# One-token attention with gMLP on one core: the gMLP's end moved between the first turn's quarters, the first turn's maximum behind the second turn's first product, and the last weight load cut at other rows

## The chip, the core and the metric

The kernel runs on one core of a Trainium2 chip. The metric is the device time of one execution, in microseconds (us). Before the change three runs gave 663.72, 664.41 and 665.36 us, median 664.41 us.

## What is computed

```python
xn = layernorm(x)                                  # x: 4 batches x 1 token x 640
q = (xn @ wq)                                      # 32 heads of 128
p = softmax(q . k_cache * 128**-0.5)               # 4096 keys for each batch and head
A = (p @ v_cache).reshape(4, 1, 4096) @ wo
z = gelu(xn @ w_in)                                # 640 -> 1728
z1, z2 = z[..., :864], layernorm(z[..., 864:])
B = (z1 * (w_sp[0, 0] * z2 + b_sp[0])) @ w_out     # 864 -> 640
out = x + A + B
```

All inputs are bf16. The two caches hold 4 x 32 x 4096 x 128 values each, 134 MB each; everything else together is about 14 MB.

## The kernel before, in words

**Turns.** The 32 heads and 4 batches are worked in 16 turns (`NT`); turn i takes one batch and 8 heads. Its keys, called K*i* here, are 8.4 MB, laid as 128 partitions of 256 keys with 128 numbers each. They are cut into four *quarters*. Its values, V*i*, are also 8.4 MB and are cut into two *parts*.

**Buffer.** SBUF holds one `ring` of 11 units (`UNITS`), a unit being the size of a quarter. K0 lies in units 4 to 7; after it odd turns' keys lie in units 0 to 3 and even turns' keys in units 3 to 6. V*i* lies in units 7 to 10, the last one, V15, in units 3 to 6. At the start units 0 to 2 hold `wq`, and units 9 and 10 hold the gMLP's weights (key `"w"`). The output weights `wo` come last, into units 0 to 2.

**Loads.** All large loads are issued by the sync engine SP in one written order (lines 189 to 198): w, K0 (two halves), K1, V0, K2, V1, K3, and so on, then V15 in two halves, then wo. `pump` (line 203) issues the next load as soon as, in the program's order, every unit it overwrites has been marked as used. At run time SP waits for the engines that used those units; SP runs its queue in order, so a load that waits holds back all behind it. K2 overwrites units 3 to 6. Unit 3 holds the last quarter of K1, which is the first one that turn 1 works, so K2 can be issued once turn 1's first quarter has been summed. V0 overwrites units 7 to 10, that is the quarter of K0 that turn 0 works first and the gMLP's weights.

**A turn.** The order on TensorE (PE), VectorE (DVE), ScalarE (ACT) and SP is that of the program, written out by hand (`manual_schedule`, line 760). For each quarter DVE multiplies the keys by the query in place (`product`, line 536) and adds the upper 64 numbers to the lower 64 (`fold`, line 545). PE then sums these 64 down to 8 with eight matmuls with the identity (`sums`, line 554); then DVE sums the 8 (`row_sums`, line 567), one quarter later. After the four quarters DVE takes the maximum (`lane_max`, line 576), ACT and PE spread it over the lanes (lines 578, 580), DVE reduces it (`exps`, line 586), ACT takes the exponential (line 590) and deals it out into the weights for the values' matmuls (`deal`, line 601). The values' matmuls of turn i-1 (`blocks`, line 629) and their gathering (`gather`, lines 642, 646) stand behind the second and third quarter of turn i.

**Before the turns** come the query projection (line 340), the query's spreading (`stage_q`), and the gMLP: its input matmuls (`gmlp_in`, line 399), the gelu (lines 410 to 427), the statistics (lines 436 to 454), and in `gmlp_out` the gate's two factors (lines 463 to 468 on DVE, 477 on PE, 481 on ACT), the gated product (lines 483 to 495 on DVE) and 18 output matmuls (line 499). These add into a bank that also holds x. `keep_rest` (line 670) copies this bank to SBUF in turn 0, behind its second quarter; its copy is read only at the end, by `open_finals` (line 680).

**The end.** The last turn's output runs through `blocks`, `gather`, `group_norm`, `group_turn` and `group_pick`, then `pair_proj(0)` and `pair_proj(1)` multiply by wo: 16 rows r, four matmuls each (line 751). The wo load of the second pair is cut at `WO_CUTS` (line 166). The result leaves by lines 817 to 821.

Of the kernel before, what the change touches and what calls it, by code (L numbers as in the profile page):

```python
# [20 lines left out]
def kernel(  # L21
# [83 lines left out]
    def quarters(i):  # L105
        return tuple(range(NQ)) if place_k(i) == K_EVEN else tuple(reversed(range(NQ)))
# [54 lines left out]
    HP = 2 * HT  # L161
# [1 line left out]
    LP = P // HP  # L163
    wo_r = A_wo.rearrange("(j p r) n -> j p (r n)", p=P, r=HP)
    wo_tiles = {}
    WO_CUTS = (0, 12 * D, 15 * D, HP * D)
    WO_UNITS = -(-NP * HP * D // UNIT)

    def load_wos():
# [33 lines left out]
    def pump():  # L203
        while loads:
            keys, first, fn, args = loads[0]
            spots = range(first, first + len(keys))
            for u, key in zip(spots, keys):
                if u in holder and holder[u] != key and holder[u] not in used:
                    return
            holder.update(zip(spots, keys))  # L210
            fn(*args)
            loads.pop(0)
# [242 lines left out]
            out=rst_t, in_=var_t, func=ACT.Sqrt, bias=eps_tile[:1], scale=1.0  # L455
        )

    def gmlp_out():
        z3, st, ac = (gm[n] for n in ("z3", "st", "ac"))
        mean_t = st[:, 0:Bsz]  # L460
        rst_t = st[:, 3 * Bsz : 4 * Bsz]
        tmp_t = st[:, 4 * Bsz : 5 * Bsz]
        nc.vector.reciprocal(out=rst_t, in_=rst_t)
        nc.vector.tensor_scalar(
            out=ac[:, 0:Bsz], in0=rst_t, scalar1=wsp_t[:, 0:1], scalar2=None, op0=ALU.mult
        )
        nc.vector.tensor_tensor(out=tmp_t, in0=ac[:, 0:Bsz], in1=mean_t, op=ALU.mult)
        nc.vector.tensor_scalar(
            out=ac[:, Bsz : 2 * Bsz],
            in0=tmp_t,  # L470
            scalar1=-1.0,
            scalar2=bsp_t[:, 0:1],
            op0=ALU.mult,
            op1=ALU.add,
        )
        ac_ps = ps_m.tile([P, 2 * Bsz], FP32, tag="m", name="ac_ps")
        nc.tensor.matmul(
            out=ac_ps[:], lhsT=ones_row[:], rhs=ac[:], start=True, stop=True
        )
        ac_sb = work.tile([P, 2 * Bsz], FP32, name="ac_sb")  # L480
        nc.scalar.copy(out=ac_sb[:], in_=ac_ps[:])
        gate = z3[:, 2, :, :]
        nc.vector.tensor_tensor(
            out=gate,
            in0=z3[:, 1, :, :],
            in1=ac_sb[:, None, 0:Bsz].to_broadcast([P, NFC, Bsz]),
            op=ALU.mult,
        )
        nc.vector.tensor_tensor(
            out=gate,  # L490
            in0=gate,
            in1=ac_sb[:, None, Bsz : 2 * Bsz].to_broadcast([P, NFC, Bsz]),
            op=ALU.add,
        )
        nc.vector.tensor_tensor(out=gm["yT"][:], in0=z3[:, 0, :, :], in1=gate, op=ALU.mult)
        for k in range(NFC):
            w = P if k < NFF else TN
            for half in range(2):
                nc.tensor.matmul(
                    out=out_sum(half),  # L500
                    lhsT=gm["yT"][:w, k, :],
                    rhs=w_out_sb[:w, k, half * NOH : (half + 1) * NOH],
                    start=False,
                    stop=(k == NFC - 1),
                )
# [28 lines left out]
    def product(i, q):  # L534
        t = quarter(i, q)
        nc.vector.tensor_tensor(  # L536
            out=t,
            in0=t,
            in1=qbcs[i // Bsz][:, i % Bsz, None, :].to_broadcast([P, QC, Dh]),
            op=ALU.mult,  # L540
        )

    def fold(i, q):
        t = quarter(i, q)
        nc.vector.tensor_tensor(  # L545
            out=t[:, :, 0:HD2], in0=t[:, :, 0:HD2], in1=t[:, :, HD2:Dh], op=ALU.add
        )
# [16 lines left out]
    def row_sums(i, q):  # L564
        if i not in scores:
            scores[i] = small.tile([P, NC], FP32, name="s_sb")
        nc.vector.tensor_reduce(  # L567
            out=scores[i][:, q * QC : (q + 1) * QC],
            in_=sums_ps.pop((i, q))[:],
            axis=AX.X,  # L570
            op=ALU.add,
        )

    def lane_max(i):
        m1 = small.tile([P, 1], FP32, name="m1")
        nc.vector.tensor_reduce(out=m1[:], in_=scores[i][:], axis=AX.X, op=ALU.max)  # L576
        d = small.tile([P, LN], FP32, name="lay")
        nc.scalar.activation(out=d[:], in_=lane_diag[:], func=ACT.Copy, scale=m1[:, 0:1])  # L578
        ps = ps_m.tile([P, LN], FP32, tag="m", name="max_ps")
        nc.tensor.matmul(out=ps[:], lhsT=head_scale[:], rhs=d[:], start=True, stop=True)  # L580
        maxes[i] = ps

    def exps(i):
        hg, b = divmod(i, Bsz)
        nb = small.tile([P, 1], FP32, name="nb")
        nc.vector.tensor_reduce(  # L586
            out=nb[:], in_=maxes.pop(i)[:], axis=AX.X, op=ALU.max, negate=True
        )
        p = probs[i] = small.tile([P, NC], BF16, name="p")
        nc.scalar.activation(  # L590
            out=p[:],
            in_=scores.pop(i)[:],
            func=ACT.Exp,
            bias=nb[:],
            scale=scale_qk,
            accum_out=acc[hg % NACC][:, b : b + 1],
        )
# [41 lines left out]
    def gather(i):  # L639
        hg, b = divmod(i, Bsz)  # L640
        pv_sb = work.tile([P, GC * Dh], FP32, tag="once", name="pv_sb")
        nc.scalar.copy(out=pv_sb[:], in_=pv_acc[:])  # L642
        if b == 0:
            pvs[hg] = ps_pv.tile([P, HT, Bsz], FP32, tag="pv", name="pv")
        for k in range(GC):
            nc.tensor.matmul(  # L646
                out=pvs[hg][:, :, b],
                lhsT=pv_sb[:, k * Dh : (k + 1) * Dh],
                rhs=sel[:, k, :],
                start=(k == 0),  # L650
                stop=(k == GC - 1),
            )
# [14 lines left out]
    def keep_rest():  # L667
        for half in range(2):
            ps = slice(OG * half, OG * half + Bsz)
            nc.vector.tensor_copy(out=rest[ps], in_=out_sum(half))  # L670
# [89 lines left out]
    with tc.manual_schedule(engines={E.PE, E.DVE, E.Activation, E.SP}):  # L760
        pump()
        stage_q(0)
        gmlp_in()
        gmlp_gelu()
        gmlp_stats()
        gmlp_out()
        used.add("w")
        pump()
        LAST = NT - 1
        for i in range(NT):  # L770
            order = quarters(i)
            ends = i // Bsz - 1 if i > Bsz and i % Bsz == 1 else None
            for n, q in enumerate(order):
                product(i, q)
                fold(i, q)
                if n:
                    row_sums(i, order[n - 1])
                if ends is not None and n == 1:
                    group_rden(ends)
                    group_norm(ends)  # L780
                elif ends is not None and n == 2:
                    group_pick(ends)
                sums(i, q)
                if i % Bsz == Bsz - 1 and n == 1 and i // Bsz + 1 < HG:
                    stage_q(i // Bsz + 1)
                if ends is not None and n < 2:
                    (group_den, group_turn)[n](ends)
                if i == 0 and n == 1:
                    keep_rest()
                if i and n in (1, 2):  # L790
                    blocks(i - 1, n - 1)
                    if n == 2:
                        gather(i - 1)
            row_sums(i, order[-1])
            lane_max(i)
            if i == LAST:
                open_finals()
            exps(i)
            if i == LAST:
                group_den(HG - 1)  # L800
                deal_part(i, 0)
                deal_part(i, 1)
            else:
                deal(i)
        assert not loads
        group_rden(HG - 1)
        blocks(LAST, 0)
        blocks(LAST, 1)
        gather(LAST)
        group_norm(HG - 1)  # L810
        group_turn(HG - 1)
        group_pick(HG - 1)
        for j in range(NP):
            pair_proj(j)

        res = work.tile([P, NOH], BF16, name="res")
        nc.scalar.copy(out=res[:OUT, 0:NOQ], in_=finals[0][column_half(0), 0:NOQ])
        nc.vector.tensor_copy(out=res[:OUT, NOQ:NOH], in_=finals[1][column_half(1), 0:NOQ])
        out_v = out.flatten_outer_dims()
        nc.scalar.dma_start(out=out_v[:, NOH:D], in_=res[OG : OG + Bsz])  # L820
        nc.sync.dma_start(out=out_v[:, 0:NOH], in_=res[0:Bsz])
# [30 lines left out]
```

## Time and profile before

| what | value |
|---|---|
| median of 3 runs | 664.41 us (663.72 to 665.36) |
| the profiled execution | 664.25 us, of which the span is 662.2 us |
| DVE busy | 497.0 us (75%) |
| PE busy | 316.2 us (48%) |
| ACT, POOL busy | 86.0 us, 8.4 us |
| DMA moved | 282.56 MB, mean 427 GB/s |
| mean granted TensorE clock | 0.71 of full speed |

The profile is one execution. Times in it count from the start of the span; about 2 us of the execution's time lie outside the span. "Busy" is the time in which an engine executes instructions; waiting is not busy. SPq and DVEq are the engines' queues, where DMAs are issued and semaphores are waited for. In a timeline row the columns are start (us), duration (us), engine, line, operation, output and inputs with shapes; in brackets stands how long the engine was idle before, and what released it. In a row of stretches there stand the stretch, its length, the busy time of each engine with the number of instructions, the granted clock, the DMA engines' busy share, and the GB/s moved.

### The profile page before, as it was taken

To read this page: it belongs to the slowest core of one execution; us is meant where nothing else is said; L and a number is where in the kernel's file an instruction comes from. 1 tells how busy PE (TensorE), PEld (TensorE's weight loads), DVE (VectorE), ACT (ScalarE), POOL (GpSimd) and SP (SyncE) were. 2 spreads that over 40 slices of the span, in tenths; PEclk is the share of its full clock that TensorE was granted. 3 is DMA by queue.
4 is the path that set the end of the run, shared out by engine and by line. 5 is a ranking of instruction groups with operands and counts; after the bars stand their busy time and mean duration, and the time that the engine had idled before them with its cause. 6 is when DMAs were issued, how large, how long until landed. Compare 5 with 4: busy or idle time off the path is not lost.

```text
span 662.2 us, 4881 instructions
## 1 busy us (share of the span) xinstructions
PE 316.2 (48%) x2095; PEld 144.8 (22%) x2095; DVE 497.0 (75%) x287; ACT 86.0 (13%) x208; POOL 8.4 (1%) x31
## 2 busy tenths in 40 slices
PE   0654372707436272644717175362715537361576
PEld 0411130302213030221303032130301213121134
DVE  2298988949497795949769496977939598794961
ACT  0400302020201102020110202001020200202000
POOL 3000000000000000000000000000000000000000
PEclk9998686765767576576757656675766868666686
DMA  9999999999999999999999999999999999999996
GB/s 369 438 452 439 404 413 431 436 444 424 444 428 425 435 435 440 431 440 428 428 436 431 439 429 443 428 432 439 432 428 435 433 435 436 439 431 425 420 425 262
DMA packets 5993, 282.56 MB, mean 427 GB/s; under 512 B 680, under 2 KB 820, under 8 KB 1108
## 3 DMA queue, kind: packets, MB, share of 16 engines
q1 hardware_dynamic: 5952, 282.24, 98.8%
q8 instruction: 16, 0.26, 0.1%
q14 instruction: 5, 0.04, 0.0%
q10 hardware_dynamic: 20, 0.01, 0.0%
HBM read 282.24 MB, written 0.01 MB: 426 GB/s over the span
## 4 chain that ended last, share of the span: by engine, by line
DMA 71%; PE 19%; DVE 8%; ACT 1%; issue 1%; SPq 0%; DVEq 0%
DMA ring<-in_A_v_cache_dram 66%; PE pv_acc L629 11%; PE s_ps L554 6%; DVE ring L536 5%; DMA ring<-in_A_wo_dram 3%; DVE ring L545 2%; DMA ring<-in_A_wq_dram 2%; PE q_ps L340 1%; PE zT L399 0%; DVE s_sb L567 0%; PE s_ps L751 0%; ACT ring L389 0%; PE pv L646 0%; DVE rest L670 0%; DVE q_sb L347 0%
## 5 line engine op out<-in xcount | busy, mean ns | idle before, releaser
L536 DVE TENSOR_TENSOR ring<-ring,qbc 128x8192 bf16<-128x8192 bf16 x64 | 282.8, 4418 | 72.3 <-DMA ring<-in_A_k_cache_dram 72.2
L554 PE MATMUL s_ps<-ring,ident 128*128 128x512 bf16 x512 | 184.9, 526 | 249.2 <-DVE ring L545 249.2
L545 DVE TENSOR_TENSOR ring<-ring 128x4096 bf16<-128x4096 bf16 x64 | 146.7, 2292 | 2.2
L554 PEld LDWEIGHTS <-ident 128*128 128x128 bf16 x512 | 62.9, 127 | 355.2 <-issue 261.3
L629 PE MATMUL pv_acc<-ring,pm 128*32 128x512 bf16 x1024 | 85.2, 491 | 30.2 <-DMA ring<-in_A_v_cache_dram 30.2
L567 DVE TENSOR_REDUCE s_sb<-s_ps 128x64 f32<-128x512 f32 x64 | 43.9, 686 | 35.9 <-PE s_ps L554 35.8
L629 PEld LDWEIGHTS <-pm 128*32 128x32 bf16 x1024 | 45.1, 148 | 66.5 <-issue 58.4
L642 ACT COPY pv_sb<-pv_acc 128x512 f32<-128x512 f32 x16 | 9.4, 586 | 358.0 <-PE pv_acc L629 358.0
L601 ACT ACTIVATE pm<-p,hmask 128x256 bf16<-128x256 bf16 x120 | 49.5, 494 | 0.5
L646 PE MATMUL pv<-sel,pv_sb 128*128 128x8 f32 x128 | 16.9, 259 | 11.1 <-ACT pv_sb L642 11.1
L646 PEld LDWEIGHTS pv<-sel,pv_sb 128*128 128x128 f32 x128 | 15.5, 191 | 18.4 <-ACT pv_sb L642 18.4
L578 ACT ACTIVATE lay<-lane_diag,m 128x16 f32<-128x16 f32 x16 | 4.9, 308 | 109.9 <-DVE m L576 109.9
L580 PE MATMUL max_ps<-lay,head_scale 128*128 128x16 f32 x32 | 6.5, 280 | 25.3 <-ACT lay L578 25.3
L580 PEld LDWEIGHTS max_ps<-lay,head_scale 128*128 128x128 f32 x32 | 5.0, 196 | 34.9 <-ACT lay L578 34.9
L586 DVE TENSOR_REDUCE nb<-max_ps 128x1 f32<-128x16 f32 x16 | 2.8, 175 | 12.9 <-PE max_ps L580 12.9
L692 POOL TENSOR_TENSOR own_sum<-acc,hmask 128x32 f32<-128x32 f32 x4 | 2.0, 498 | 625.2 <-ACT p L590 625.2
L590 ACT ACTIVATE p<-s_sb,nb 128x256 bf16<-128x256 f32 x16 | 8.1, 507 | 10.8 <-DVE nb L586 10.8
L522 ACT CAST q_rows<-qr_ps 32x128 bf16<-32x128 f32 x4 | 1.0, 256 | 59.7 <-PE qr_ps L514 59.7
L576 DVE TENSOR_REDUCE m<-s_sb 128x1 f32<-128x256 f32 x16 | 6.7, 420 | 0.5
L709 DVE TENSOR_TENSOR o_n<-pv,rden 128x32 bf16<-128x32 f32 x4 | 0.8, 191 | 7.8 <-PE pv L646 7.7
L340 PE MATMUL q_ps<-ring,xnT 128*32 128x512 bf16 x40 | 4.5, 630 | 3.7 <-DMA ring<-in_A_wq_dram 3.7
L324 PE MATMUL xnT_ps<-ident,xn_bf 4*128 4x4 bf16 x5 | 0.4, 178 | 11.5 <-DVE xn_bf L312 11.5
(95 smaller groups left out, 86.5 us busy)
## 6 DMA issues: line engine op xcount, KB each, us to landing
ring<-in_A_k_cache_dram SPq DMA_DIRECT2D x2, 4096.0 KB, 28.1
ring<-in_A_v_cache_dram SPq DMA_DIRECT2D x2, 4096.0 KB, 28.2
ring<-in_A_wq_dram SPq DMA_DIRECT2D x1, 5120.0 KB, 15.2
ring<-in_A_wo_dram SPq DMA_DIRECT2D x1, 2560.0 KB
ring<-in_B_w_in_dram SPq DMA_DIRECT2D x1, 2160.0 KB, 19.8
ring<-in_A_wo_dram SPq DMA_DIRECT2D x1, 1920.0 KB
ring<-in_B_w_out_dram SPq DMA_DIRECT2D x1, 960.0 KB, 21.7
ring<-in_A_wo_dram SPq DMA_DIRECT2D x1, 480.0 KB, 18.4
```

The costliest lines, as they stand in the source:

```text
L340: nc.tensor.matmul(out=q_ps[hg // CG][g * QW : (g + 1) * QW, :], lhsT=xnT[:, c, :], rhs=wq_sb[:, c, hg * QH * Dh : (hg + 1) * QH * Dh], st ...
L536: nc.vector.tensor_tensor(out=t, in0=t, in1=qbcs[i // Bsz][:, i % Bsz, None, :].to_broadcast([P, QC, Dh]), op=ALU.mult,)
L545: nc.vector.tensor_tensor(out=t[:, :, 0:HD2], in0=t[:, :, 0:HD2], in1=t[:, :, HD2:Dh], op=ALU.add)
L554: nc.tensor.matmul(out=s[:], lhsT=ident[:], rhs=t[:, :, g * RW : (g + 1) * RW], start=(g == 0), stop=(g == n - 1),)
L567: nc.vector.tensor_reduce(out=scores[i][:, q * QC : (q + 1) * QC], in_=sums_ps.pop((i, q))[:], axis=AX.X, op=ALU.add,)
L576: nc.vector.tensor_reduce(out=m1[:], in_=scores[i][:], axis=AX.X, op=ALU.max)
L580: nc.tensor.matmul(out=ps[:], lhsT=head_scale[:], rhs=d[:], start=True, stop=True)
L590: nc.scalar.activation(out=p[:], in_=scores.pop(i)[:], func=ACT.Exp, bias=nb[:], scale=scale_qk, accum_out=acc[hg % NACC][:, b : b + 1],)
L601: nc.scalar.activation(out=p_m[i % 2][:, :, h, :], in_=probs[i][:].rearrange("p (n c) -> p n c", c=BC), func=ACT.Copy, scale=hmask[:, h : ...
L629: nc.tensor.matmul(out=pv_acc[g * CW : (g + 1) * CW, :], lhsT=pm[:, b0 // BC, :, :].rearrange("p h (k c) -> p c (h k)", k=GC)[:, c, :], rh ...
L642: nc.scalar.copy(out=pv_sb[:], in_=pv_acc[:])
L646: nc.tensor.matmul(out=pvs[hg][:, :, b], lhsT=pv_sb[:, k * Dh : (k + 1) * Dh], rhs=sel[:, k, :], start=(k == 0), stop=(k == GC - 1),)
```

## The change

- `gmlp_out` is cut in two. `gmlp_gate` holds the gate's factors (lines 463 to 481 of before) and now runs in turn 0 behind the first quarter's fold, ahead of that quarter's sums. The rest, still called `gmlp_out` (lines 483 to 499), runs in turn 0 behind the second quarter's sums, and with it the mark that the gMLP's weights are used, and `pump`.
- `keep_rest` moves from turn 0's second quarter to turn 2's second quarter.
- Turn 0's last `row_sums` and its `lane_max` move behind turn 1's first product and ahead of its fold; `exps` and `deal` of turn 0 follow behind that fold. Other turns stay as they were.
- The last wo load is cut in pieces of 11, 4 and 1 rows in place of 12, 3 and 1.

The instructions of each engine are the same ones, in another order; on SP only the sizes of two wo pieces differ.

```diff
-    WO_CUTS = (0, 12 * D, 15 * D, HP * D)
+    WO_CUTS = (0, 11 * D, 15 * D, HP * D)
...
-    def gmlp_out():
-        z3, st, ac = (gm[n] for n in ("z3", "st", "ac"))
+    def gmlp_gate():
+        st, ac = gm["st"], gm["ac"]
...
         nc.scalar.copy(out=ac_sb[:], in_=ac_ps[:])
+        gm["ac_sb"] = ac_sb
+
+    def gmlp_out():
+        z3, ac_sb = gm["z3"], gm["ac_sb"]
         gate = z3[:, 2, :, :]
...
         gmlp_stats()
-        gmlp_out()
-        used.add("w")
-        pump()
         LAST = NT - 1
         for i in range(NT):
             order = quarters(i)
             ends = i // Bsz - 1 if i > Bsz and i % Bsz == 1 else None
+            late = i - 1 if i == 1 else None
             for n, q in enumerate(order):
                 product(i, q)
+                if n == 0 and late is not None:
+                    row_sums(late, quarters(late)[-1])
+                    lane_max(late)
                 fold(i, q)
+                if i == 0 and n == 0:
+                    gmlp_gate()
                 if n:
                     row_sums(i, order[n - 1])
+                elif late is not None:
+                    exps(late)
+                    deal(late)
...
                 if i == 0 and n == 1:
+                    gmlp_out()
+                    used.add("w")
+                    pump()
+                elif i == 2 and n == 1:
                     keep_rest()
...
+            if i == 0:
+                continue
             row_sums(i, order[-1])
             lane_max(i)
```

## The prediction

> **What bounds the kernel now.** I read the page first: its span, its fourth part (the chain that ended last) and its DMA rows.
>
> ```profile
> span 662.2 us, 4881 instructions
> DMA  9999999999999999999999999999999999999996
> GB/s 369 438 452 439 404 413 431 436 444 424 444 428 425 435 435 440 431 440 428 428 436 431 439 429 443 428 432 439 432 428 435 433 435 436 439 431 425 420 425 262
> DMA 71%; PE 19%; DVE 8%; ACT 1%; issue 1%; SPq 0%; DVEq 0%
> ```
>
> The DMA engines are busy in every slice, and the chain is mostly DMA. DVE, busy 75%, waits for them. So a change on DVE or PE gains only where a transfer starts late enough to leave the DMA engines short of work. The GB/s row has such a place: slices 5 and 6 (66 to 99 us) move 404 and 413. I took that region in equal stretches.
>
> ```profile
> 64.00:77.00 13.00, 4.50 (x13) 1.60 (x12) 9.87 (x6) 5.49 (x12) 0.00 (x0) 0.63 0.99 429
> 77.00:90.00 13.00, 8.03 (x49) 2.99 (x48) 12.93 (x7) 0.00 (x0) 0.00 (x0) 0.78 0.98 384
> 90.00:103.00 13.00, 7.64 (x55) 3.56 (x52) 8.07 (x6) 1.97 (x6) 0.00 (x0) 0.87 1.00 434
> ```
>
> Against 434 GB/s, the stretch 77 to 90 lost 13 x (1 - 384/434) = **1.5 us**. Now the timeline with the issues there, what waited for K2, and the group row of all K loads.
>
> ```profile
> 44.32 0.33 SPq L157 DMA_DIRECT2D ring<-in_A_v_cache_dram  x1
> 78.69 0.33 SPq L152 DMA_DIRECT2D ring<-in_A_k_cache_dram  x1
> 103.19 4.42 DVE L536 TENSOR_TENSOR ring<-ring,qbc 128x8192 bf16<-128x8192 bf16 x1 [1.33 <-DMA ring<-in_A_k_cache_dram]
> DMA to landing us min/median/max: 24.5/28.2/28.5
> ```
>
> K2 is issued at 78.69 and lands at 103.19: 24.5 us, the least of all K loads, where the median is 28.2. One load is 8.39 MB, at 434 GB/s 19.3 us. So a usual K waits 28.2 - 19.3 = 8.9 us in the queue behind the V ahead of it. K2 had 24.5 - 19.3 - 1.5 = **3.7 us**, and only there the flow breaks. Working back (estimates): V0 landed at 103.19 - 1.5 - 19.3 = 82.4, K1 at 63.1. I read it so: an issue 3.7 us before the queue runs out is too late by what the break cost.
>
> **What lead suffices** is seen at the end, where wo is issued behind V15.
>
> ```profile
> 626.99 3.64 PE L629 MATMUL pv_acc<-ring,pm 128*32 128x512 bf16 x32 [3.22 <-DMA ring<-in_A_v_cache_dram]
> 638.74 2.05 SPq L175 DMA_DIRECT2D ring<-in_A_wo_dram  x4
> 652.74 2.25 PE L751 MATMUL s_ps<-ring,o_r 128*4 128x160 bf16 x64
> 657.16 2.31 PE L751 MATMUL s_ps<-ring,o_r 128*4 128x160 bf16 x64 [2.18 <-DMA ring<-in_A_wo_dram]
> ring<-in_A_wo_dram SPq DMA_DIRECT2D x1, 2560.0 KB
> ring<-in_A_wo_dram SPq DMA_DIRECT2D x1, 1920.0 KB
> ring<-in_A_wo_dram SPq DMA_DIRECT2D x1, 480.0 KB, 18.4
> ```
>
> V14 lands at 626.99, so V15 at 626.99 + 19.3 = 646.3, and wo was issued 7.6 us ahead. From 626.99 to 657.16 the queue moved V15, 2560 KB and 1920 KB, 12.98 MB in 30.2 us, 430 GB/s: no break. So 3.7 us lost 1.5, and 7.6 us lost nothing.
>
> **The change: when K2 is issued.** It waits for turn 1's first fold and its sums. The DVE rows up to there:
>
> ```profile
> 30.91 0.15 DVE L453 TENSOR_TENSOR st<-st 1x4 f32<-1x4 f32 x1
> 31.42 0.17 DVE L463 RECIPROCAL st<-st 1x4 f32<-1x4 f32 x1 [0.36 <-ACT st L454]
> 32.06 0.22 DVE L468 TENSOR_SCALAR ac<-st,bsp_t 1x4 f32<-1x4 f32 x1
> 33.22 0.20 DVE L483 TENSOR_TENSOR z<-z,ac_sb 128x36 f32<-128x36 f32 x1 [0.95 <-ACT ac_sb L481]
> 33.81 4.42 DVE L536 TENSOR_TENSOR ring<-ring,qbc 128x8192 bf16<-128x8192 bf16 x1
> 44.93 2.29 DVE L545 TENSOR_TENSOR ring<-ring 128x4096 bf16<-128x4096 bf16 x1
> 47.28 3.57 PE L554 MATMUL s_ps<-ring,ident 128*128 128x512 bf16 x8 [3.09 <-DVE ring L545]
> 47.74 0.97 DVE L670 COPY rest<-out_ps 4x320 f32<-4x320 f32 x2
> 62.79 0.68 DVE L567 TENSOR_REDUCE s_sb<-s_ps 128x64 f32<-128x512 f32 x1
> 66.23 0.69 DVE L567 TENSOR_REDUCE s_sb<-s_ps 128x64 f32<-128x512 f32 x1 [2.76 <-PE s_ps L554]
> 66.96 0.42 DVE L576 TENSOR_REDUCE m<-s_sb 128x1 f32<-128x256 f32 x1
> 68.30 4.42 DVE L536 TENSOR_TENSOR ring<-ring,qbc 128x8192 bf16<-128x8192 bf16 x1
> 72.75 2.29 DVE L545 TENSOR_TENSOR ring<-ring 128x4096 bf16<-128x4096 bf16 x1
> ```
>
> Step 1, the head. The first product stands at 33.81 behind the gate and its output. After the change DVE is free at 31.1, but the keys' first half must have landed. These rows place it:
>
> ```profile
> 15.93 4.46 PE L340 MATMUL q_ps<-ring,xnT 128*32 128x512 bf16 x40 [3.67 <-DMA ring<-in_A_wq_dram]
> ring<-in_B_w_in_dram SPq DMA_DIRECT2D x1, 2160.0 KB, 19.8
> ring<-in_B_w_out_dram SPq DMA_DIRECT2D x1, 960.0 KB, 21.7
> ring<-in_B_w_out_dram SPq DMA_DIRECT2D x2, 60.0 KB
> ring<-in_A_k_cache_dram SPq DMA_DIRECT2D x2, 4096.0 KB, 28.1
> ```
>
> Behind wq (landed 15.9) come 2160 + 960 + 2 x 60 + 4096 KB, 7.5 MB, 17.3 us: 33.2. So the head gains 33.81 - 33.2 = 0.6 us, not the 2.7 that DVE is free earlier.
>
> Step 2, what is put in: the gate's four DVE operations, 31.42 to 32.28, 0.86 us; the output's three, 33.22 to 33.81, 0.6 us. Step 3, keep_rest goes: -1.0 (its 0.97 and the gap behind). The row_sums of 62.79 then stands at 62.79 - 0.6 + 0.86 + 0.6 - 1.0 = 62.65, and turn 1's product 0.7 later, 63.3, just behind K1's landing at 63.1. Step 4: the wait of 2.76 us for the last sums lies beside this product; it ends at 67.8, then row_sums and maximum (0.69 + 0.42), fold from 68.9 to 71.2. Before, the fold ended at 75.04 and K2 went out 3.65 later; so now at **74.9**, 3.8 us earlier and 82.4 - 74.9 = 7.5 us ahead of V0's landing. The nearest row is wo's 7.6, which lost nothing, so I take the whole 1.5 us. Bounds: 0 (the break has another cause) and 1.65 (the stretch before, at 429, counted too: 0.15 more).
>
> By the Trainium skill, DMA: Bandwidth & Descriptors, section Specifications, a DMA issued from the sync engine needs about 0.6 us to its first byte. By that, K2's 3.7 us would have been plenty, and the sum would hold only the last cut; the trace's break in just this place speaks against reading it so.
>
> **What is late next.** V0 waits for the gMLP's output matmuls, now on PE behind the second quarter's sums.
>
> ```profile
> 33.93 2.65 PE L499 MATMUL out_ps<-ring,yT 128*4 128x320 bf16 x18 [0.95 <-DVE yT L495]
> 69.67 3.30 ACT L601 ACTIVATE pm<-p,hmask 128x256 bf16<-128x256 bf16 x8
> 142.66 4.43 DVE L536 TENSOR_TENSOR ring<-ring,qbc 128x8192 bf16<-128x8192 bf16 x1 [7.16 <-DMA ring<-in_A_k_cache_dram]
> DVE ring L536 <- DMA ring<-in_A_k_cache_dram: 72.2, 14, 7.8
> ```
>
> The second fold ended at 47.2 and ends at 47.5 now (-0.6 + 0.86); sums 3.6, matmuls 2.65: V0 is issued at 53.8, not 44.32. Behind it on SP stand K2 and all later loads. It is 63.1 - 53.8 = 9.3 us ahead of K1's landing, more than wo's 7.6: cost nothing. The output's operands are ready at 47.5 + 0.7 + 0.6 = 48.8, under the sums. The gate stands ahead of the first sums on PE. The first fold ends at 33.2 + 4.42 + 2.29 = 39.9; the gate's DVE part takes 0.86, and matmul and copy at most the 0.94 from 32.28 to their reader at 33.22. So these sums run from 41.7 to 45.3; they are read at 47.5: 2 us of cover, and the stall only begins beyond it. Turn 0's deal ends some 3 us later than its 72.97, near 76, and its first reader waits for V0 at 82.4: 6 us of cover. keep_rest costs turn 2's DVE 1.0 us, covered by the wait for K3, 7.16 us; over all turns DVE waits 72.2 us for keys in 14 times. None is on the path, so the 1.5 us goes through to the end.
>
> **The last cut.** The final 64 matmuls wait for the first piece; then they run at 2.31/64 = 36 ns without a stop. One row less is 160 KB, 0.16 MB at 434 GB/s = **0.38 us** earlier. The 4-row piece lands where the 3-row one did, 480 KB (1.1 us) behind 657.12; PE needs it 44 x 36 ns = 1.6 us after 656.78, at 658.4, 0.1 us of cover; the last row has 0.3. The first pair's matmuls end at 654.99, 1.8 us ahead. If the second piece is late, the gain shrinks to 0; past that none is lost, as its landing does not move. I take 0.38.
>
> **Sum.** 664.25 - 1.5 - 0.38 = 662.4 for the profiled execution. The median lies 0.16 higher, so 662.5: 0.29% faster. About 0.3%, 2.0 us, is what a measurement of this kernel tells from no change; the forecast sits at that edge.
>
> **Rivals.**
> - *The break stays*: it comes from something else between 77 and 90 us, or 7.5 us still is too little. For: I infer the cause from one place. Against: every load with a longer lead flows on. Time 664.41 - 0.38 = 664.0. The 0.6 us of the Trainium skill's page named above lead here too.
> - *Only the break goes*: the 4-row piece gates the end and the cut brings nothing: 664.41 - 1.5 = 662.9. For: 0.1 us of cover.
> - *Slower*: V0 is the load that comes late. If PE reaches the 18 matmuls late, SP holds V0 back and all behind it. By K2's rows the break costs 1.5 us at an issue 3.7 us before the queue's end, here 59.4, and a microsecond more for each one later. The change is undone from 59.8, and from 61.8 it is over 0.3% slower: 666.4 and up, say 666.8. Against: I find 53.8, and the sums ahead took 3.57 us.
>
> **How the numbers follow.** Forecast 0.76, break stays 0.11, only the break goes 0.07, slower 0.06. The forecast case spreads by about 0.6 us, from the spread of the three runs (663.72 to 665.36) and the bounds of the 1.5; a little under half of it passes 2.0 us: faster 0.36. Within: 0.58, the rest of the forecast and both smaller rivals. Slower 0.06. Range 661.7 to 664.1: below by the 1.65 bound (0.15) and half the run spread (0.7 or so), above to the stayed break.
>
> **What would show it.** K2's issue near 74.9 with V0's at 53.8; the least K time to landing 26.8 us or more; 77 to 90 near 430 GB/s; DVE's first wait for keys ending near 101.7 in place of 103.19; the last 64 matmuls starting near 655.3. Wrong if 77 to 90 still moves 384 with K2 issued early, if 50 to 70 now breaks, or if the last matmuls show a wait inside.

## The result and the profile after

| | before | after |
|---|---|---|
| median | 664.07 us (6 runs, 663.29 to 665.36) | 661.50 us (6 runs, 661.40 to 661.68) |
| ratio, 95% interval | | 0.996 [0.9947, 0.9973] |
| profiled execution, its span | 664.25 us, 662.2 us | 661.40 us, 659.4 us |

The change saves 2.57 us by the medians and 2.85 us between the two profiled executions. The forecast was 662.5 us, the range began at 661.7 us: the time fell 0.2 us below it. The page of the changed kernel has these rows in the place of those of before:

```profile
span 659.4 us, 4881 instructions
DMA  8999999999999999999999999999999999999997
GB/s 369 432 459 438 417 438 437 430 442 430 429 437 426 433 442 433 437 430 421 437 438 441 437 431 417 437 434 437 442 429 425 443 421 434 441 433 438 419 419 297
DMA 78%; PE 19%; DVE 2%; issue 1%; SPq 0%; POOL 0%; ACT 0%; POOLq 0%
```

Slices 5 and 6, which moved 404 and 413 GB/s, now move 417 and 438, and DVE's share of the chain fell from 8% to 2%: before, the chain ran through DVE's work of turns 0 and 1 up to the issue of V1 at 92.83 us; now it follows the transfers of K0 and V0 there, with only the 19.3 us from the first product to V0's issue on the engines. The stretches of 13 us show the same:

```profile
64.00:77.00 13.00, 6.71 (x17) 2.46 (x16) 12.93 (x7) 5.50 (x12) 0.00 (x0) 0.63 0.98 423
77.00:90.00 13.00, 10.91 (x80) 4.56 (x79) 12.97 (x6) 0.00 (x0) 0.00 (x0) 0.63 1.03 445
90.00:103.00 13.00, 4.86 (x22) 2.48 (x19) 5.64 (x7) 4.79 (x12) 0.00 (x0) 0.63 0.98 423
```

77 to 90 moves 445 GB/s in place of 384. The timeline of the changed kernel around turn 0's end and K2's issue, and the group row of the K loads:

```profile
34.02 4.42 DVE L540 TENSOR_TENSOR ring<-ring,qbc 128x8192 bf16<-128x8192 bf16 x1 [2.79 <-DMA ring<-in_A_k_cache_dram]
51.09 2.09 PE L503 MATMUL out_ps<-ring,yT 128*4 128x320 bf16 x18
53.32 0.33 SPq L157 DMA_DIRECT2D ring<-in_A_v_cache_dram  x1
63.79 4.41 DVE L540 TENSOR_TENSOR ring<-ring,qbc 128x8192 bf16<-128x8192 bf16 x1
68.12 0.68 DVE L571 TENSOR_REDUCE s_sb<-s_ps 128x64 f32<-128x512 f32 x1
68.84 0.42 DVE L580 TENSOR_REDUCE m<-s_sb 128x1 f32<-128x256 f32 x1
69.18 2.28 DVE L549 TENSOR_TENSOR ring<-ring 128x4096 bf16<-128x4096 bf16 x1
75.11 0.33 SPq L152 DMA_DIRECT2D ring<-in_A_k_cache_dram  x1
82.66 3.64 PE L633 MATMUL pv_acc<-ring,pm 128*32 128x512 bf16 x32 [0.83 <-DMA ring<-in_A_v_cache_dram]
101.93 4.42 DVE L540 TENSOR_TENSOR ring<-ring,qbc 128x8192 bf16<-128x8192 bf16 x1 [3.70 <-DMA ring<-in_A_k_cache_dram]
DMA to landing us min/median/max: 26.8/28.1/29.4
```

V0 goes out at 53.32 (53.8 was forecast), K2 at 75.11 (74.9), V0 lands at 82.66 (82.4), K2 at 101.93 (101.7). The K load that was quickest from issue to landing takes 26.8 us, as forecast, in place of 24.5. So the mechanism came as predicted to within 0.3 us. But K2 lands only 103.19 - 101.93 = 1.26 us earlier, and the end comes 2.85 us earlier. The rest appears later. Four waits for landings of the changed kernel, K3, K9, V14 and wo's first piece:

```profile
140.52 4.43 DVE L540 TENSOR_TENSOR ring<-ring,qbc 128x8192 bf16<-128x8192 bf16 x1 [3.83 <-DMA ring<-in_A_k_cache_dram]
...
372.31 4.42 DVE L540 TENSOR_TENSOR ring<-ring,qbc 128x8192 bf16<-128x8192 bf16 x1 [6.45 <-DMA ring<-in_A_k_cache_dram]
...
624.75 2.71 PE L633 MATMUL pv_acc<-ring,pm 128*32 128x512 bf16 x32 [2.33 <-DMA ring<-in_A_v_cache_dram]
...
654.28 2.34 PE L755 MATMUL s_ps<-ring,o_r 128*4 128x160 bf16 x64 [1.87 <-DMA ring<-in_A_wo_dram]
```

K3 lands 142.66 - 140.52 = 2.14 us earlier than before, V14 626.99 - 624.75 = 2.24, wo's first piece 657.16 - 654.28 = 2.88, of which 0.38 is its smaller size. So about 2.5 us, not 1.5, reached the end by way of the loads.

### The profile page after: what moved, and what is told of

It reads as the page before. It is cut to its first block, busy times and chain, and to the rows that moved or that the text cites. A ratio compares the mean times of both kernels' runs of the same rounds, so it can differ in the third digit from the quotient of the medians.

```text
span 659.4 us, 4881 instructions
## 1 busy us (share of the span) xinstructions
PE 320.2 (49%) x2095; PEld 147.6 (22%) x2095; DVE 496.6 (75%) x287; ACT 86.0 (13%) x208; POOL 8.4 (1%) x31
## 4 chain that ended last, share of the span: by engine, by line
DMA 78%; PE 19%; DVE 2%; issue 1%; SPq 0%; POOL 0%; ACT 0%; POOLq 0%
DMA ring<-in_A_v_cache_dram 70%; PE pv_acc L633 12%; PE s_ps L558 6%; DMA ring<-in_A_k_cache_dram 5%; DMA ring<-in_A_wo_dram 3%; DVE ring L540 1%; DVE ring L549 1%; PE s_ps L755 0%; PE out_ps L503 0%; PE pv L650 0%; SPq L141 0%; ACT pv_sb L646 0%; SPq L175 0%; DVE res L834 0%; POOL ident masks.py:199 0%
## 5 line engine op out<-in xcount | busy, mean ns | idle before, releaser
L558 PE MATMUL s_ps<-ring,ident 128*128 128x512 bf16 x512 | 186.8, 531 | 232.3 <-DVE ring L549 232.3
L584 PE MATMUL max_ps<-lay,head_scale 128*128 128x16 f32 x32 | 7.2, 301 | 26.8 <-ACT lay L582 26.8
```

Source lines behind the costliest of these rows:

```text
L558: nc.tensor.matmul(out=s[:], lhsT=ident[:], rhs=t[:, :, g * RW : (g + 1) * RW], start=(g == 0), stop=(g == n - 1),)
```

## The experiments

**Theory A.** The late issue of K2 makes the break, and the break costs more than the data that did not flow in it, because the 16 DMA engines lose unequal amounts there and the last landing waits for the one that is farthest behind. **Theory B.** The break is worth the 1.5 us of the stretches, and the rest came from the cut of the last load. **Rival C.** Not K2's issue but the gMLP's move carries part of the gain.

**e1_cut_only**: before, with the cut alone.

```diff
-    WO_CUTS = (0, 12 * D, 15 * D, HP * D)
+    WO_CUTS = (0, 11 * D, 15 * D, HP * D)
```

> The kernel before with only the last weight load cut at 11, 4 and 1 rows. Theory A (the break of the flow near 80 us is worth about 2.2 us because it also sets the 16 DMA engines apart, and the cut is worth the 0.38 us worked out): about 0.4 us under the kernel before, 663.7 us. Theory B (the break is worth the 1.5 us that the stretches show, and the cut brings the rest of the 2.57 us): about 1.1 us under it, 663.0 us.

Measured: 663.65 us, ratio 0.9993 [0.9984, 1.0001]. **e2_old_cut** is the changed kernel with that line turned back.

> The changed kernel with the old cut of 12, 3 and 1 rows. Theory A: 0.4 us over the changed kernel, 661.9 us, 2.2 us under the kernel before. Theory B: 1.1 us over it, 662.6 us.

Measured: 661.74 us, ratio 0.9963 [0.9951, 0.9976]. Both put the cut at about 0.25 us (663.91 - 663.65, and 661.74 - 661.50), and the rest of the change at 2.2 us. Theory B falls: the cut has not even its 0.38 us, though for a quarter of a microsecond the comparisons are too coarse to be sure of its size.

**e3_max_only**: the gMLP back ahead of the turns, keep_rest back in turn 0, the old cut; only the maximum behind turn 1's first product is left.

```diff
         gmlp_stats()
+        gmlp_gate()
+        gmlp_out()
+        used.add("w")
+        pump()
...
-                if i == 0 and n == 0:
-                    gmlp_gate()
...
                 if i == 0 and n == 1:
-                    gmlp_out()
-                    used.add("w")
-                    pump()
-                elif i == 2 and n == 1:
                     keep_rest()
```

> Only turn 0's last sums and maximum behind turn 1's first product; the gMLP stays ahead of the turns, keep_rest in turn 0, the old cut. Theory A with the issue of K2 as the cause: K2 is issued near 75.0 us and the whole break goes: 661.9 us, as with the gMLP moved too. Rival (the gMLP's move carries part of the gain): 662.5 us or more.

Measured: 661.64 us, ratio 0.9962 [0.9948, 0.9975], K2 issued at 74.99. **e4_gmlp_only** is the other half: the gMLP between the quarters and keep_rest in turn 2, the maximum where it was, the old cut.

```diff
-            late = i - 1 if i == 1 else None
+            late = None
...
-            if i == 0:
-                continue
             row_sums(i, order[-1])
```

> Only the gMLP's gate and output between turn 0's quarters and keep_rest in turn 2; the maximum stays where it was, the old cut. If the first product starts with the landing of the first keys at 34.0 us (0.2 later than before) and 1.5 us go in and 1.0 out: K2 issued near 79.3 us, the break stays or grows, 664.1 to 664.9 us. If the head gains the 0.6 us of the prediction: K2 near 78.5 us, 664.0 us. Rival (the gMLP's move carries half of the gain): 663 us or less.

Measured: 663.75 us, ratio 0.9994 [0.9985, 1.0003].

```profile
33.96 4.43 DVE L540 TENSOR_TENSOR ring<-ring,qbc 128x8192 bf16<-128x8192 bf16 x1 [3.10 <-DMA ring<-in_A_k_cache_dram]
79.56 0.33 SPq L152 DMA_DIRECT2D ring<-in_A_k_cache_dram  x1
```

The first product waits for the keys until 33.96, so the head gains nothing, the gMLP's operations are in turn 0's way, and K2 is issued 0.9 us later than before. The gMLP's move by itself brings nothing that can be told from no change; rival C falls.

**How late is too late.** e5, e6 and e7 are the changed kernel with one DVE reduction ahead of turn 1's first fold. Its result goes nowhere; it only makes K2's issue late. R is 14, 28 and 60.

```diff
+    idle = work.tile([P, R], FP32, name="idle")
+
+    def stall():
+        nc.vector.tensor_reduce(
+            out=idle[:],
+            in_=ident_f[:, None, :].to_broadcast([P, R, P]),
+            axis=AX.X,
+            op=ALU.add,
+        )
...
                     lane_max(late)
+                    stall()
                 fold(i, q)
```

> The changed kernel with one extra DVE reduction of about 1.9 us ahead of turn 1's first fold, whose result nobody reads. K2 is issued near 77.0 us, 5.4 us ahead of V0's landing. If a lead is either enough or not and 5.4 us is enough: 661.5 us as the changed kernel. If the loss falls off evenly between 3.7 and 7.4 us of lead: about 1.2 us more, 662.7 us. If the lead of K2 is not the cause at all: 661.5 us here and in the next two kernels.

Measured: 661.62 us, ratio 0.9966 [0.9954, 0.9979].

> The same with a reduction of about 3.7 us: K2 is issued near 78.9 us, as late as in the kernel before, with everything else as in the changed kernel. Theory A (the late issue makes the break, and the break costs 2.2 us because it sets the 16 DMA engines apart): 663.7 us, with a run scatter of 1 us or more again. Theory B (the break is worth 1.5 us): 663.0 us. If it is not the issue of K2 that counts: 661.5 us.

Measured: 663.80 us, ratio 0.9994 [0.9985, 1.0003], runs from 662.22 to 664.46.

> The same with a reduction of about 8 us: K2 is issued near 83.2 us, after V0 has landed, so that all 16 DMA engines stand empty and start together. A price of a microsecond for each microsecond of lateness on top of the break: 661.5 + 2.2 + 4.3 = 668 us. If starting together takes away the scatter that the break leaves, less: K2 lands near 83.2 + 1.7 + 19.3 = 104.2 us, 2.3 later than in the changed kernel, and with a slow start of up to 1 us the time is 664 to 665 us, with little scatter.

Measured: 666.23 us, ratio 1.0037 [1.0024, 1.0049], runs from 666.00 to 666.75. K2's issue in e5, then K2's issue and the stretch 77 to 90 in e6, with its wait for K2, and in e7:

```profile
76.91 0.33 SPq L152 DMA_DIRECT2D ring<-in_A_k_cache_dram  x1
```

```profile
78.58 0.33 SPq L152 DMA_DIRECT2D ring<-in_A_k_cache_dram  x1
77.00:90.00 13.00, 8.85 (x49) 3.17 (x48) 12.93 (x7) 1.98 (x5) 0.00 (x0) 0.62 0.97 394
102.76 4.43 DVE L540 TENSOR_TENSOR ring<-ring,qbc 128x8192 bf16<-128x8192 bf16 x1 [1.49 <-DMA ring<-in_A_k_cache_dram]
```

```profile
83.03 0.33 SPq L152 DMA_DIRECT2D ring<-in_A_k_cache_dram  x1
77.00:90.00 13.00, 7.40 (x32) 2.69 (x35) 12.97 (x7) 3.90 (x10) 0.00 (x0) 0.55 0.78 314
```

e6 settles that K2's issue makes the break: the order is that of the changed kernel, K2's issue is back where it was, and the gain but for that of the cut is gone, with the scatter back as well. The reduction also makes DVE's work of turn 1 late, but DVE still waits 1.49 us for K2 at its end, so this is not what costs the time. Why the break costs more than the data, the second half of Theory A, is taken up further down. e5 costs nothing. In e7 K2 is issued after V0's landing; it costs 4.7 us. That is more than the expectation of 664 to 665 us and less than 668 us. By the packet records its first packets start 1.0 us after the start of the issue, not 1.7.

**e10_rest_only**: before, with keep_rest in turn 2 and nothing else.

```diff
-                if i == 0 and n == 1:
+                if i == 2 and n == 1:
                     keep_rest()
```

> The kernel before with only keep_rest moved to turn 2. K2 is issued near 77.7 us, 4.7 us ahead of V0's landing. If the edge lies under 4.7 us of lead: 661.9 us (the old cut), with little scatter. If the edge lies between 4.7 and the 5.5 us that were enough: between 662.3 and 664.0 us.

Measured: 661.78 us, ratio 0.9968 [0.9956, 0.998].

```profile
77.81 0.33 SPq L152 DMA_DIRECT2D ring<-in_A_k_cache_dram  x1
77.00:90.00 13.00, 8.94 (x54) 3.13 (x56) 12.93 (x7) 0.00 (x0) 0.00 (x0) 0.65 1.01 435
```

This one moved copy, 0.97 us of DVE, brings all that the change brings but the cut. K2 at 77.81 flows on, K2 at 78.58 breaks.

**e9_stall_turn8**: the changed kernel with the reduction (R is 44, 6.01 us on DVE) in turn 8, to see whether the place matters.

```diff
+                if i == 8 and n == 0:
+                    stall()
                 fold(i, q)
```

> The changed kernel with an extra DVE reduction of about 6.0 us, whose result nobody reads, ahead of the first fold of turn 8 instead of turn 1. K9's issue, usually 8.9 us ahead of V7's landing, then comes about 2.9 us ahead of it. If any transfer issued that late breaks the flow: 663.7 to 665 us, with a scatter of 1 us or more. If only the first loads are touchy: 661.5 us.

Measured: 663.05 us, 1.55 us above the changed kernel, runs from 661.47 to 663.94. K9's issue and its landing:

```profile
349.73 0.33 SPq L152 DMA_DIRECT2D ring<-in_A_k_cache_dram  x1
373.79 4.42 DVE L540 TENSOR_TENSOR ring<-ring,qbc 128x8192 bf16<-128x8192 bf16 x1 [1.19 <-DMA ring<-in_A_k_cache_dram]
```

K9 lands at 373.79 instead of 372.31. So a late issue breaks the flow in the middle too; the loss is less than expected, and its scatter the largest of all.

**e8_four_cuts** and **e11_rest_four_cuts**: the changed kernel, and the kernel of e10, with the last load in pieces of 10, 3, 2 and 1 rows.

```diff
+    WO_CUTS = (0, 10 * D, 13 * D, 15 * D, HP * D)
```

> The changed kernel with the last weight load cut at 10, 3, 2 and 1 rows. The first piece lands 0.38 us earlier than with 11 rows, and the 64 matmuls then wait for the last pieces instead: about 0.2 us less, 661.3 us. If a fourth piece costs as much as it brings: 661.5 us.

Measured: 661.36 us, ratio 0.9962 [0.995, 0.9974].

> The kernel before with only keep_rest moved to turn 2 and the last weight load cut at 10, 3, 2 and 1 rows: two one-line edits, without the gMLP's and the maximum's move. If the break's going and the end of the last load are all that counts: as the changed kernel with the four cuts, 661.4 us. If K2's 4.6 us of lead holds only just: single runs near 663 us among them.

Measured: 661.52 us, ratio 0.9958 [0.9945, 0.9972], runs from 661.45 to 661.62, K2 at 78.04. The last matmuls of e8:

```profile
653.76 0.86 PE L755 MATMUL s_ps<-ring,o_r 128*4 128x160 bf16 x40 [2.51 <-DMA ring<-in_A_wo_dram]
654.89 0.57 PE L755 MATMUL s_ps<-ring,o_r 128*4 128x160 bf16 x12 [0.27 <-DMA ring<-in_A_wo_dram]
655.69 0.77 PE L755 MATMUL s_ps<-ring,o_r 128*4 128x160 bf16 x12 [0.22 <-DMA ring<-in_A_wo_dram]
```

They start half a microsecond earlier and then wait twice for pieces, 0.5 us together; the end moves from 656.62 to 656.46. e8 has the lowest median of all, 0.14 us under the changed kernel, which is less than these runs can tell. e11 does with two one-line edits what the whole change does.

**All kernels side by side.** The lead is 82.66 (V0's landing in the changed kernel; in the others it differs by at most 0.2) less K2's issue, read from one execution of each. The last column is from the trace's packet records: by how much the 128 packets of the last one-row piece end, on average, ahead of the last of them.

| kernel | K2's issue, lead (us) | runs (us) | average to last (us) |
|---|---|---|---|
| before | 78.69, 4.0 | 663.29 to 665.36 | 2.4 |
| e1_cut_only | 79.26, 3.4 | 662.28 to 664.04 | 2.2 |
| e4_gmlp_only | 79.56, 3.1 | 662.64 to 664.22 | 1.8 |
| e6_stall4 | 78.58, 4.1 | 662.22 to 664.46 | 2.8 |
| e11_rest_four_cuts | 78.04, 4.6 | 661.45 to 661.62 | 1.5 |
| e10_rest_only | 77.81, 4.9 | 661.62 to 661.95 | 1.2 |
| e5_stall2 | 76.91, 5.8 | 661.55 to 661.82 | 1.4 |
| after | 75.11, 7.6 | 661.40 to 661.68 | 1.4 |
| e3_max_only | 74.99, 7.7 | 661.25 to 661.84 | 1.3 |
| e2_old_cut | 74.89, 7.8 | 661.56 to 661.81 | 1.2 |
| e8_four_cuts | 74.65, 8.0 | 661.30 to 661.54 | 1.3 |
| e7_stall8 | 83.03, -0.4 | 666.00 to 666.75 | 1.7 |

The kernels fall in three groups. With 4.6 us of lead or more the flow goes on, and all runs of a kernel lie within 0.6 us. From 4.1 down to 3.1 us it breaks, at a price of about 2 us that hardly grows with the lateness, and single runs lie 1.6 to 2.2 us apart (e1, e4 and e6 ran 11 times, the kernels without the break 5 or 6 times; more runs alone spread somewhat wider). With no lead at all all engines stand still, it costs 4.7 us, and the runs agree within 0.8 us again.

## Why the prediction was wrong, step by step

- **What bounds the kernel, and where it can be changed**: right. e6 shows that K2's issue alone makes and undoes the break.
- **Head gains 0.6 us**: wrong, by the landing. The first keys were placed at 33.2 and came at 34.0, so the head lost 0.2 us. Turn 1's product came 0.5 us behind the forecast, its fold 0.3, K2's issue 0.2.
- **7.5 us of lead suffice**: right, and far more than needed: the edge lies between 4.1 us (e6) and 4.6 us (e11). K2's own lead before was 4.0 us by V0's landing, not 3.7. The forecast had only bounds of 3.7 and 7.6 and took the safe one; it did not see that one of the change's parts alone, keep_rest's 1.0 us, would cross the edge.
- **The break is worth 1.5 us, bounds 0 and 1.65**: this is the step that failed. The removal is worth 2.2 us (e2) to 2.3 us (e3, and e6 against after). I took the data that did not flow for the delay of the end. The two are different, as the amounts still to move late in the kernel show (before, then after; the last column is GB/s):

```profile
630.00:650.00 20.00, 15.85 (x140) 7.21 (x132) 10.51 (x11) 1.49 (x4) 1.28 (x1) 0.77 0.99 423
650.00:660.00 10.00, 6.26 (x156) 5.57 (x152) 2.28 (x4) 0.87 (x2) 0.00 (x0) 0.64 0.59 245
```

```profile
630.00:650.00 20.00, 14.55 (x149) 8.21 (x149) 8.62 (x13) 2.08 (x5) 1.28 (x1) 0.82 0.97 418
650.00:660.00 10.00, 4.64 (x128) 3.99 (x127) 1.91 (x3) 0.28 (x1) 0.00 (x0) 0.50 0.45 188
```

After 630 us the kernel before moves 20 x 423 + 10 x 245 = 10,910 kB, the changed one 20 x 418 + 10 x 188 = 10,240 kB. The difference, 670 kB, is 1.54 us at 434 GB/s: the 1.5 us of the forecast were right as an amount of data. Yet the last landings came 2.5 us earlier. The missing 1.0 us is the distance between the average engine and the last one: the packets of the last piece end on average 2.4 us ahead of the last one before, 1.4 us after. A landing is reported when the last of the 16 engines is done. The Trainium skill says as much of the counting (DMA: Bandwidth & Descriptors, section Why a DMA increments its semaphore by 16 and not by 1): the engines finish independently, and only the full count means that all data has landed.

The packet records also tell when this distance arises, for each large load ends with 16 writes of 4 bytes, one from each engine. By these, the average engine ends K2 1.47 us later before than after, and V14 still 1.45 us later: the data's 1.5 us are lost at K2 and stay lost (in e6 it is 1.0 us at both). The last engine lies behind the average by (us):

| kernel | V0 | K2 | K3 | K6 | K12 | K15 | V14 |
|---|---|---|---|---|---|---|---|
| before | 1.44 | 1.18 | 1.85 | 1.59 | 2.51 | 2.21 | 2.21 |
| e6_stall4 | 1.44 | 1.24 | 1.12 | 2.13 | 1.64 | 2.76 | 2.76 |
| after | 1.44 | 1.35 | 1.22 | 0.95 | 1.58 | 1.32 | 1.32 |

At K2 the last engine is no farther behind with the break than without it (in e1 and e4 it is, with 1.79 and 1.70), so Theory A is right that a landing waits for the engine that is farthest behind, but the rest is not lost at K2. The last engine falls back later, in single steps. The usual distance between two landings is 19.32 us; before, K3 comes 0.80 us and K12 1.30 us later than that, in e6 K6 1.27 and K15 1.42. In each case a packet of 16 KB from another queue went out shortly ahead, at 126.3 and 475.5 us before, at 247.2 and 601.1 in e6: the queue q8, which the page's list of DMA queues names `instruction` (packets, MB, share of 16 engines; the row of before).

```profile
q8 instruction: 16, 0.26, 0.1%
```

Such a packet runs on one engine alone, takes 0.9 to 1.0 us, and the next packet of 64 KB on that engine takes 2.9 in place of 2.42 us: 1.4 us for that engine. Followed from packet to packet, each starting where the one ahead of it ended, the two packets of before lie on the engine that is last at K3 and K12. The changed kernel has 16 such packets too, but the engine that is last at V0 stays last up to K9, with a landing every 19.32 us, and the packets fall on engines ahead of it; it falls back by only 0.84 us at V8 and 0.29 at K10. With the break another engine is last after K2 than at V0. That the break does its further harm by changing the order of the engines is read from one execution of each kernel; no run here moves the instruction packets, so this last link is not shown by a run of its own, nor is it shown that the scatter comes from it.

- **V0's later issue costs nothing**: right, 53.32 and no new break. **keep_rest is covered in turn 2**: right (e10). **The cut, 0.38 us**: about 0.25 us, a size that these runs can't tell from 0.38 with certainty.
- **The rival "break stays"** fell; an issue 4.1 us ahead of the queue's end was too late (e6). That also decides against reading it by the 0.6 us to the first byte of the Trainium skill (DMA: Bandwidth & Descriptors, section Specifications): by the packet records the first packet of K2 starts 0.6 us behind the end of its issue in e7, so the trace agrees with that figure, but it does not give the lead that suffices while the queue is full. **The slower rival** did not come; its price, a microsecond for each microsecond of lateness on top of 1.5, would have put e7 at 1.5 + 4.3 = 5.8 us above, and 4.7 were measured.
- **The range** took its lower bound from the same 1.5 us and the scatter of the runs before. That scatter was itself a sign of the break: it went with it.

## What to carry to other kernels

Where loads follow each other without a pause, look for the one issue that comes with the least lead, and move it only as far as the edge needs: here one copy of 1 us in another turn did the work of the whole rearrangement. A landing waits for the slowest DMA engine, so a hole in the flow can delay the end by more than the average that GB/s rows show, here 2.2 us against 1.5; price it from the shift of later landings. A kernel whose runs scatter more than its relatives' may have such a hole.

## What was unexpected of the hardware

- The edge is sharp: K2's issue at 78.04 us costs nothing, at 78.58 us about 2 us. By the packet records of the kernel before, the engines finish V0 between 80.0 and 82.2 us, so the lead over the first of them is 2.2 us less than the lead over V0's landing, and the first packets of K2 start 1.4 us after the start of its issue; in the first 4 us after the break packets of 64 KB take up to 4.2 us, where 2.42 us is usual, which makes 1.1 of the 1.5 us lost.
- Of a break's cost, the smaller part shows at the transfer concerned (e6: K2 lands at 102.76, 0.83 us later than in the changed kernel), the larger part only at later landings (2.5 us at V14, 627.23 against 624.75).
